# A hand-kept order table of 1,528 operations is replaced by another, with other engines for some of them

## Chip, core and metric

The kernel runs on one core of one Trainium2 chip. The metric is device time in microseconds (us), the median of several executions. Five engines matter: TensorE (PE, with PEld for its weight loads), VectorE (DVE), ScalarE (ACT), GpSimd (POOL) and the DMA queue of SyncE (SP).

## The reference, cut to what matters

Attention over chunks of 32 queries with 16 keys to the left, 8 to the right and 8 memory keys, for 4 batches of 8 heads, followed by a feed-forward block with a gate made by a 3-tap convolution over the sequence:

```python
scores = scale * np.matmul(q_c, k_full.transpose(0, 1, 3, 2))
a = np.exp(scores - np.max(scores, axis=-1, keepdims=True))
a = a / (np.sum(a, axis=-1, keepdims=True) + 1e-09)
out[:, :, c_start:c_end] = np.matmul(a, v_full)
...
h = np.maximum(x @ w_in, 0.0)                      # 512 -> 1024
conv_out = sum(conv_w[k] * hp[:, k:k + S, :] for k in range(3))
gate = 1.0 / (1.0 + np.exp(-conv_out))
return (h * gate @ w_out).astype(np.float32)       # 1024 -> 512
```

q is 4 x 8 x 768 x 64. The weights arrive as 64-bit floats in the kernel's buffers and are split on the chip into a rounded high part and a low part.

## The kernel before, in words

Everything stays in one recorded plan. `attention(n)` records the work of one of 32 pieces (4 batches x 2 halves of the sequence x 4 pairs of heads; "piece 20" below is n = 20): three loads, 24 score matmuls into PSUM tile `s` (L381), a maximum on VectorE (L390), the softmax, a sum and its reciprocal (L422, L424), a normalising multiplication (L427), a turn of the weights (three transposes on TensorE, L439, with copies L446, or a VectorE transpose L457 with two DMAs), 24 value matmuls into `ta` (L486), and the split of the result into a high part (ACT L489) and a low part (DVE L492).

`ffn_in(b, fc, hf)` multiplies the four results of a half by one block of 128 channels of `w_in`, as hi*hi + lo*hi + hi*lo, three matmuls of 384 columns each (L508), into a PSUM tile `f`, which ACT empties with a relu (L518). Four such tiles exist. `gated(b, fc)` makes the gate of a channel block ("block 1,6" is batch 1, fc 6): the middle tap (L528 on ACT or L532 on DVE), two more taps on DVE (L537, 128 x 767), a sigmoid on ACT (L541), the multiplication h * gate (L545 on DVE or GpSimd), a rounded high part (ACT L549) and the low part (L552 on DVE or GpSimd). `ffn_out(b, tt)` multiplies all eight blocks of a batch by `w_out` (L564) and stores the rows (L575 and a DMA). `from_f64` splits the weights (L276 to L348) in one of several kinds, chosen by a letter.

Which engine takes an optional operation stands in strings with one letter for each piece or block. `TAP` (A or V) is the middle tap, `MULT` and `LO` (V = VectorE, G = GpSimd) are L545 and L552, `NORM` is L427, `SOFT` is V for one VectorE subtraction (L395) and one ACT exponential (L401), or A for a small VectorE scaling (L407) and six ACT exponentials (L413). `W_IN`, `W_OUT` and `W_CONV` are the kinds of split. `KEEP` and `HOME` choose buffers.

The list `ORDER` gives the sequence in which the recorded operations are emitted. Each engine runs its own instructions in that sequence and waits where an operand or a buffer is not ready. Nothing is reordered on the chip. A buffer goes to the operation that comes next in `ORDER` once the last user of the buffer has been emitted. The numbers in `ORDER` are places in the recording, so the list moves whole operations, their DMAs included. No planner runs in the kernel: the arguments `cost`, `shared`, `late`, `gap` and so on of `Plan.op` are not read when the plan runs. `shared=True` marks what the author took to use the port that VectorE and GpSimd have in common: L280, L286, L293, L301, L306, L312, L348, L407, L427, L532, L537, L545, L552.

Of the kernel before, what the change touches and what calls it, by code (L numbers as in the profile page):

```python
# [29 lines left out]
W_IN, W_OUT, W_CONV = "SMMSmMCM", "CmMMCMMM", "R"  # L30
TAP = "AAAAAAVAAAAAAAAAAVAVAVAAVAAAAAAA"
MULT = "VGGVGGGGGVGGGGGGVVGVVVVVVGVGVVGG"
LO = "VGGVVVVVVVGGGGVGVVVGGVGVVGGGGVVG"
SOFT = "AVVAAAAVAVVAVVVAVVVAVVVVVVAAAVAV"
NORM = "GGVVGGVGGGGGVGGGVVVGVVVVVGVGVVGV"
KEEP = "KKKKKNNKKKKKKNKKNKKNNKKNKNKNNNNK"
HOME = "wwwwwwwwwwwwwwwwwwxxwwwwwxxxwxxx"
# [73 lines left out]
]  # L111


# [578 lines left out]
```

## Time and profile before

| what | value |
|---|---|
| three executions | 362.62, 363.25, 363.29 us, median 363.25 |
| the profiled execution | 362.65 us, of which the span of its instructions is 360.9 us |
| PE busy | 339.0 us (94%) in 2955 matmuls |
| DVE busy | 255.5 us (71%) in 431 instructions |
| ACT busy, POOL busy | 215.5 us (60%), 100.4 us (28%) |
| granted TensorE clock, mean | 0.995 |

The profiled execution lies 1.75 us above its span and 0.6 us under the median. Shares of busy time are averages over stages with different limits: VectorE is nearly always busy in the first 200 us and almost idle in the last 45, and TensorE is the reverse. So the windows have to be read by stage. A matmul's end is modelled, so "PE busy" in a window says where TensorE waited and not how fast it ran.

### The profile page before, as it was taken

The page shows a single profiled execution, that of the slowest core. Times are in us where ns is not written, and L with a number is a line of the kernel's source. Part 1 is how long each engine was busy: PE and PEld are TensorE (multiplying, and loading weights), DVE is VectorE, ACT ScalarE, POOL GpSimd, SP SyncE. Part 2 cuts the span into 40 slices and gives each one's busy share as a digit, 9 for nine tenths or more (in the row PEclk, how much of TensorE's full clock was granted, in tenths as well). Part 3 has the DMA queues.
Part 4 walks back from the last instruction along what each step waited for, and adds up shares of the span by engine and source line. Part 5 has one row for each costly group of instructions (what it writes and reads, how often), then busy time and mean ns, then how long its engine had stood idle before and what let it go on. Part 6 is the DMA issues. An engine that isn't in the chain of part 4 may idle for free.

```text
span 360.9 us, 7378 instructions
## 1 busy us (share of the span) xinstructions
PE 339.0 (94%) x2955; PEld 299.6 (83%) x2955; DVE 255.5 (71%) x431; ACT 215.5 (60%) x401; POOL 100.4 (28%) x75
## 2 busy tenths in 40 slices
PE   1799999999989978799999999999999999999996
PEld 1679899879979977789988789988998888888886
DVE  4999999999999999999999828350645997300000
ACT  2567888699988958755749786322579623311011
POOL 3314121292424355520002064000004596400000
PEclk9999999999999999899999999999999999999999
DMA  8998947866748545352065383512000110201012
GB/s 287 404 396 279 345 153 250 256 216 218 251 143 261 184 141 205 98 174 91 0 226 184 122 255 111 171 58 91 2 0 0 40 53 26 88 29 58 31 58 87
DMA packets 26386, 54.50 MB, mean 151 GB/s; under 512 B 3056, under 2 KB 13168, under 8 KB 26352
## 3 DMA queue, kind: packets, MB, share of 16 engines
q1 hardware_dynamic: 26352, 54.04, 44.2%
q8 instruction: 23, 0.38, 0.4%
q14 instruction: 11, 0.09, 0.1%
HBM read 44.79 MB, written 9.24 MB: 150 GB/s over the span
## 4 chain that ended last, share of the span: by engine, by line
PE 58%; DVE 22%; issue 2%; ACT 2%; POOL 0%; ACTq 0%; POOLq 0%; DVEq 0%
PE f L564 38%; PE f L508 16%; DVE w L537 9%; PE ta L486 2%; PE s L381 2%; DVE u L492 1%; DVE top L390 1%; DVE z L422 1%; DVE e L395 1%; DVE e L427 1%; DVE w L457 1%; DVE u L545 1%; DVE w L306 1%; DVE w L301 1%; DVE w_top L286 1%
## 5 line engine op out<-in xcount | busy, mean ns | idle before, releaser
L508 PE MATMUL f<-u,w_in_hi 128*128 128x384 f32 x512 | 143.9, 347 | 4.6 <-DVE u L492 3.1
L564 PE MATMUL f<-w_out_hi,u 128*128 128x512 f32 (+1 forms) x400 | 125.7, 388 | 0.0
L508 PEld LDWEIGHTS f<-u,w_in_hi 128*128 128x128 f32 x512 | 94.0, 190 | 9.9 <-DVE u L492 5.0
L564 PEld LDWEIGHTS f<-w_out_hi,u 128*128 128x128 f32 x400 | 74.1, 188 | 16.0
L508 PE MATMUL f<-u,w_in_lo 128*128 128x384 f32 x256 | 86.8, 339 | 0.0
L537 DVE SCALAR_TENSOR_TENSOR w<-u,cw,w 128x767 f32<-128x767 f32 x64 | 80.6, 1268 | 4.1 <-ACT w L528 3.3
L564 PE MATMUL f<-w_out_lo,u 128*128 128x512 f32 (+1 forms) x200 | 77.2, 386 | 0.0
L575 ACT COPY w_top<-f 128x512 f32<-128x512 f32 (+1 forms) x25 | 14.3, 570 | 61.0 <-PE f L564 60.4
L508 PEld LDWEIGHTS f<-u,w_in_lo 128*128 128x128 f32 x256 | 48.7, 190 | 0.7
L518 ACT ACTIVATE u<-f 128x384 f32<-128x384 f32 x64 | 30.6, 491 | 23.7 <-PE f L508 23.6
L564 PEld LDWEIGHTS f<-w_out_lo,u 128*128 128x128 f32 x200 | 37.6, 188 | 7.3
L545 POOL TENSOR_TENSOR u<-w,u 128x768 f32<-128x768 f32 x12 | 26.0, 2166 | 61.3 <-ACT w L541 59.4
L541 ACT ACTIVATE w<-w 128x768 f32<-128x768 f32 x32 | 26.9, 844 | 16.2 <-DVE w L537 16.1
L486 PEld LDWEIGHTS ta<-a_d,w 128*64 128x64 f32 x768 | 24.9, 140 | 5.6 <-ACT a_d L446 2.2
L486 PE MATMUL ta<-a_d,w 128*64 128x64 f32 x768 | 27.7, 227 | 1.9 <-ACT a_d L446 1.0
L427 POOL TENSOR_TENSOR e<-e,z 128x384 f32<-128x384 f32 x16 | 15.3, 958 | 45.8 <-DVE z L424 38.3
L528 ACT ACTIVATE w<-u,cw 128x768 f32<-128x768 f32 x27 | 25.3, 937 | 3.7 <-PE s L381 2.1
L492 DVE TENSOR_TENSOR u<-ta,u 128x384 fp32r<-128x384 f32 x32 | 17.4, 548 | 12.0 <-ACT u L489 11.8
L381 PE MATMUL s<-k,w 128*64 128x64 f32 x672 | 24.7, 227 | 1.0 <-DVE e L395 1.0
L381 PEld LDWEIGHTS s<-k,w 128*64 128x64 f32 x672 | 22.1, 141 | 4.2 <-DVE e L395 1.8
L545 POOL TENSOR_TENSOR w<-w,u 128x768 f32<-128x768 f32 x6 | 13.1, 2188 | 40.0 <-ACT w L541 40.0
L552 POOL TENSOR_TENSOR u<-u,u 128x768 fp32r<-128x768 f32 x9 | 19.2, 2143 | 15.5 <-ACT u L549 14.1
(62 smaller groups left out, 368.7 us busy)
## 6 DMA issues: line engine op xcount, KB each, us to landing
w<-in_v_dram SPq DMA_DIRECT2D x32, 384.0 KB, 5.2
w<-in_q_dram SPq DMA_DIRECT2D x28, 384.0 KB, 4.6
k<-in_k_dram SPq DMA_DIRECT2D x28, 252.0 KB, 4.9
out_dram<-w_top SPq DMA_DIRECT2D x23, 256.0 KB, 2.0
w<-in_w_in_dram SPq DMA_DIRECT2D x8, 512.0 KB, 6.9
w<-in_w_out_dram SPq DMA_DIRECT2D x8, 512.0 KB, 4.1
t_dram<-w SPq DMA_DIRECT2D x15, 192.0 KB, 2.1
a_d<-t_dram SPq DMA_DIRECT2D x30, 96.0 KB, 3.3
```

The source lines that it names most:

```text
L381: nc.tensor.matmul(s.t[j * D : (j + 1) * D, o : o + KW], lhsT=q_[:, c], rhs=k_t.t[:, c * STEP : c * STEP + KW], start=True, stop=True,)
L427: lambda: (V if norm == "V" else G).tensor_tensor(out=keys(e), in0=keys(e), in1=pairs(z.t).unsqueeze(3).broadcast_to([P, NG, 2, KW]), op=A ...
L486: nc.tensor.matmul(y, lhsT=v_g[:, g, u, h], rhs=a_d.t[:, :, o], start=True, stop=True)
L492: lambda: V.tensor_tensor(out=x.t[:, TW:S], in0=a.t[:, :TW], in1=x.t[:, :TW].bitcast(F32), op=ALU.subtract), (a, (x, 0)), ((x, 1),),
L508: nc.tensor.matmul(f.t[:, :TW], lhsT=w_in_p[c][:, fc, cc], rhs=x.t[:, a * TW : (a + 1) * TW], start=(cc == 0 and i == 0), stop=(cc == NCC ...
L518: "A", act(TW, True), lambda: A.activation(h.t[:, hf * TW : (hf + 1) * TW], f.t[:, :TW], AF.Relu), (f,), ((h, hf),)
L528: plan.op("A", act(S, ptr=1), lambda: A.activation(c.t, h.t, AF.Copy, scale=w[1]), H, (c,))
L537: lambda j=j, to=to, at=at: V.scalar_tensor_tensor(out=c.t[:, to], in0=h.t[:, at], scalar=w[j], in1=c.t[:, to], op0=ALU.mult, op1=ALU.add) ...
L541: plan.op("A", act(S), lambda: A.activation(c.t, c.t, AF.Sigmoid), (c,), (c,), table="sigmoid")
L545: lambda: (V if mult == "V" else G).tensor_tensor(out=y.t, in0=c.t, in1=h.t, op=ALU.mult), (c, h), (y,), shared=True,
L552: lambda: (V if lo == "V" else G).tensor_tensor(out=g_lo.t, in0=y.t, in1=g_hi.t.bitcast(F32), op=ALU.subtract),
L564: nc.tensor.matmul(ps.t[:, :n], lhsT=gs[b, fc][a].t[:, tt * P : (tt + 1) * P], rhs=w_out_p[c][:, fc, o : o + n], start=(fc == 0 and i == 0 ...
```

## The change

All letters that choose engines and kinds, and the whole of `ORDER`, are replaced. In the letters: `W_IN` block 1 goes from M to C (its low part moves from DVE to ACT and GpSimd) and block 6 from C to M, block 4 no longer uses GpSimd for one step; the split of `conv_w` changes (one operation fewer). `SOFT` goes from 13 to 10 A, `TAP` from 5 to 7 V, `MULT` from 18 to 19 G, `LO` from 15 to 13 G, `NORM` stays at 16 G. On each engine that is: VectorE 431 to 435 operations, GpSimd 61 to 59, ScalarE 316 to 313; ScalarE's queue holds 24 loads of a function table instead of 20, and two of the four more stand before the turned weights of piece 20. TensorE's 2955 matmuls and the DMAs are the same in number and shape, in another order. `gap=380` becomes `gap=460`, an argument that nothing reads.

```diff
-W_IN, W_OUT, W_CONV = "SMMSmMCM", "CmMMCMMM", "R"
-TAP = "AAAAAAVAAAAAAAAAAVAVAVAAVAAAAAAA"
-MULT = "VGGVGGGGGVGGGGGGVVGVVVVVVGVGVVGG"
-LO = "VGGVVVVVVVGGGGVGVVVGGVGVVGGGGVVG"
-SOFT = "AVVAAAAVAVVAVVVAVVVAVVVVVVAAAVAV"
-NORM = "GGVVGGVGGGGGVGGGVVVGVVVVVGVGVVGV"
-KEEP = "KKKKKNNKKKKKKNKKNKKNNKKNKNKNNNNK"
-HOME = "wwwwwwwwwwwwwwwwwwxxwwwwwxxxwxxx"
+W_IN, W_OUT, W_CONV = "SCMSMMMM", "CmMMCMMM", "s"
+TAP = "AAAAAAVAAAVAAAAAAAVVAAAAAVAVAVAA"
+MULT = "VGGVGGGGGVVGGGGGVVGVGGGGVVGGVVVV"
+LO = "VGGGVVVVGVGVGGVGGVGVVVGGVVVVVGVV"
+SOFT = "VVVAAAAVVAVAVVVAVVVAVVVVVVVAVAVV"
+NORM = "VGVGGGGGVGGGVGGGVVVGVVVVVGVVVGGV"
+KEEP = "KKKKKNNKKKKKKNKKNKKNNKKNKKNNKNKN"
+HOME = "wwwwwwwwwwxwwwwwwwxxwwwwwxxxwxxx"
...
 ORDER = [
-    571, 12, 13, 581, 30, 29, 81, 47, 46, 572, 573, 64, 574, 63, 575, 15, 576, 577, 591, 582, 16, 14, 17, 587, 18, 583, 80,
...
+    570, 11, 12, 580, 28, 29, 45, 46, 571, 62, 572, 80, 573, 574, 63, 14, 575, 576, 591, 581, 586, 577, 15, 13, 16, 79, 582,
...
-    def op(self, eng, cost, do, r=(), w=(), shared=False, table=None, mode=None, late=70, gap=380, less=None):
+    def op(self, eng, cost, do, r=(), w=(), shared=False, table=None, mode=None, late=70, gap=460, less=None):
```

**Place A, VectorE's queue at the gates of batch 1.** Names are buffers; `w_90<-u_1269` is a pair of taps of block 1,4, then come 1,3 (`u_1204`), 1,6 (`u_1292`) and 1,5 (`u_1372`). Before:

```order
L537 SCALAR_TENSOR_TENSOR w_90<-u_1269,cw,w_90 128x767 x2
L286 TENSOR_SCALAR w_top_101<-w_top_101 128x512
L492 TENSOR_TENSOR u_1615<-ta_113,u_1615 128x384
L390 TENSOR_REDUCE top_104<-s_112 128x6
L537 SCALAR_TENSOR_TENSOR w_86<-u_1204,cw,w_86 128x767 x2
L492 TENSOR_TENSOR u_1654<-ta_114,u_1654 128x384
L395 TENSOR_TENSOR e_76<-s_112,top_104 128x3x128
L537 SCALAR_TENSOR_TENSOR w_87<-u_1292,cw,w_87 128x767 x2
L390 TENSOR_REDUCE top_105<-s_111 128x6
L395 TENSOR_TENSOR e_74<-s_111,top_105 128x3x128
L537 SCALAR_TENSOR_TENSOR w_90<-u_1372,cw,w_90 128x767 x2
```

The same place after the change (block 1,4 is `u_1229`, 1,3 is `u_1210`, 1,6 is `u_1366`; `u_1433` is block 1,2):

```order
L537 SCALAR_TENSOR_TENSOR w_86<-u_1229,cw,w_86 128x767
L537 SCALAR_TENSOR_TENSOR w_91<-u_1210,cw,w_91 128x767
L545 TENSOR_TENSOR u_1433<-w_92,u_1433 128x768
L390 TENSOR_REDUCE top_103<-s_111 128x6
L492 TENSOR_TENSOR u_1644<-ta_114,u_1644 128x384
L492 TENSOR_TENSOR u_1649<-ta_113,u_1649 128x384
L537 SCALAR_TENSOR_TENSOR w_91<-u_1210,cw,w_91 128x767
L537 SCALAR_TENSOR_TENSOR w_92<-u_1366,cw,w_92 128x767
L395 TENSOR_TENSOR e_76<-s_111,top_103 128x3x128
L390 TENSOR_REDUCE top_105<-s_112 128x6
L395 TENSOR_TENSOR e_75<-s_112,top_105 128x3x128
L537 SCALAR_TENSOR_TENSOR w_92<-u_1366,cw,w_92 128x767
```

The two taps of a block no longer stand together: the second tap of one block is followed by the first of the next and then by two or three attention operations, and the multiplication of block 1,2 is now in this queue.

**Place B, GpSimd's queue from the last step of batch 1 on.** L545 are multiplications, L552 low parts, L427 a normalisation. Before (the first row is the weight step that follows block 1,7):

```order
L343 TENSOR_TENSOR w_out_lo<-w_97 128x512
L552 TENSOR_TENSOR u_1873<-u_463,u_1576 128x768
L552 TENSOR_TENSOR u_1927<-u_606,u_1868 128x768
L545 TENSOR_TENSOR u_1940<-w_86,u_1940 128x768
L427 TENSOR_TENSOR e_74<-e_74,z_110 128x3x128
L552 TENSOR_TENSOR u_2407<-u_1269,u_2392 128x768
L552 TENSOR_TENSOR u_2453<-w_90,u_2331 128x768
L427 TENSOR_TENSOR e_74<-e_74,z_107 128x3x128
L552 TENSOR_TENSOR u_2568<-u_1435,u_2467 128x768
```

After, from the same step:

```order
L343 TENSOR_TENSOR w_out_lo<-w_97 128x512
L552 TENSOR_TENSOR u_1869<-u_465,u_1541 128x768
L552 TENSOR_TENSOR u_1914<-u_596,u_1905 128x768
L552 TENSOR_TENSOR u_1938<-u_524,u_1928 128x768
L545 TENSOR_TENSOR u_1890<-w_90,u_1890 128x768
L545 TENSOR_TENSOR w_92<-w_92,u_1797 128x768
L545 TENSOR_TENSOR u_1825<-w_89,u_1825 128x768
L427 TENSOR_TENSOR e_75<-e_75,z_110 128x3x128
L545 TENSOR_TENSOR u_1810<-w_90,u_1810 128x768
L552 TENSOR_TENSOR u_2377<-w_86,u_2362 128x768
L552 TENSOR_TENSOR u_2414<-u_1240,u_2168 128x768
L552 TENSOR_TENSOR u_2467<-u_1293,u_2453 128x768
```

One more low part stands at the front, and then four multiplications of batch 2 instead of one, in a row but for a normalisation; a fifth (block 2,4) is the next row.

## Rows read from the trace of the kernel before

**Rows 1.** The page: busy time of the engines, and the last chain's shares.

```profile
PE 339.0 (94%) x2955; PEld 299.6 (83%) x2955; DVE 255.5 (71%) x431; ACT 215.5 (60%) x401; POOL 100.4 (28%) x75
PE 58%; DVE 22%; issue 2%; ACT 2%; POOL 0%; ACTq 0%; POOLq 0%; DVEq 0%
```

**Rows 2.** Windows: their length, then busy PE, PEld, DVE, ACT, POOL, clock, DMA share, GB/s.

```profile
9.00:18.00 9.00, 6.62 (x84) 5.46 (x86) 8.62 (x19) 4.98 (x13) 3.15 (x4) 1.00 1.04 402
...
126.00:135.00 9.00, 7.19 (x79) 6.62 (x79) 8.93 (x9) 4.95 (x9) 4.51 (x2) 1.00 0.44 137
135.00:144.00 9.00, 7.50 (x67) 6.73 (x63) 8.80 (x11) 7.72 (x12) 4.90 (x2) 1.00 0.60 208
144.00:153.00 9.00, 7.04 (x34) 6.41 (x33) 8.58 (x18) 6.37 (x11) 4.33 (x3) 0.84 0.35 105
```

**Rows 3.** The chain that ended last: start, length, what.

```profile
145.81 1.87 DVE e L427
...
149.76 0.39 ACT u L518
150.19 4.95 PE f L508 x18
...
269.50 88.28 PE f L564 x402
```

**Rows 4.** VectorE's groups, 54 to 150 us: count, busy us, mean ns, idle before.

```profile
L537 DVE SCALAR_TENSOR_TENSOR w<-u,cw,w 128x767 f32<-128x767 f32 x32 | 42.3, 1326 | 0.4
...
L395 DVE TENSOR_TENSOR e<-s,top 128x384 f32<-128x384 f32 x11 | 6.1, 551 | 0.1
L427 DVE TENSOR_TENSOR e<-e,z 128x384 f32<-128x384 f32 x6 | 4.6, 772 | 0.1
...
L293 DVE SCALAR_TENSOR_TENSOR w_top<-w,w_top 128x512 uint32<-128x512 uint32 x5 | 3.4, 685 | 0.0
L545 DVE TENSOR_TENSOR u<-w,u 128x768 f32<-128x768 f32 x3 | 3.3, 1101 | 0.0
L301 DVE TENSOR_SCALAR w<-w 128x512 uint32<-128x512 uint32 x4 | 3.2, 794 | 0.0
...
L286 DVE TENSOR_SCALAR w_top<-w_top 128x512 uint32<-128x512 uint32 x4 | 2.6, 644 | 0.0
```

**Rows 5.** VectorE's groups, 153 to 211 us, where GpSimd runs six instructions.

```profile
L537 DVE SCALAR_TENSOR_TENSOR w<-u,cw,w 128x767 f32<-128x767 f32 x16 | 16.0, 1009 | 0.6 <-ACT w L528 0.4
...
L545 DVE TENSOR_TENSOR u<-w,u 128x768 f32<-128x768 f32 x3 | 2.9, 950 | 0.0
...
L286 DVE TENSOR_SCALAR w_top<-w_top 128x512 uint32<-128x512 uint32 x3 | 1.3, 417 | 0.0
```

**Rows 6.** Timeline at blocks 1,3 and 0,7: start, length, instruction, idle before.

```profile
130.16 0.84 ACT L541 ACTIVATE w<-w 128x768 f32<-128x768 f32 x1 [1.60 <-DVE w L537]
...
130.97 3.56 DVE L537 SCALAR_TENSOR_TENSOR w<-u,cw,w 128x767 f32<-128x767 f32 x2
...
131.08 2.64 POOL L545 TENSOR_TENSOR u<-w,u 128x768 f32<-128x768 f32 x1 [2.82 <-ACT w L541]
...
99.77 1.83 POOL L545 TENSOR_TENSOR u<-w,u 128x768 f32<-128x768 f32 x1
```

**Rows 7.** VectorE's groups in the first 27 us.

```profile
L348 DVE SCALAR_TENSOR_TENSOR w_in_lo<-w 128x512 fp32r<-128x512 uint32 x2 | 2.5, 1249 | 0.0
```

**Rows 8.** Timeline up to batch 3's first matmul, and later at alternating multiplications.

```profile
188.51 0.63 PE L564 MATMUL f<-w_out_hi,u 128*128 128x512 f32 x2
...
210.59 0.56 DVE L492 TENSOR_TENSOR u<-ta,u 128x384 fp32r<-128x384 f32 x1 [1.03 <-ACT u L489]
...
213.57 0.34 PE L508 MATMUL f<-u,w_in_hi 128*128 128x384 f32 x1
...
291.39 2.60 DVE L537 SCALAR_TENSOR_TENSOR w<-u,cw,w 128x767 f32<-128x767 f32 x1
```

**Rows 9.** ScalarE's timeline at the sigmoid of block 1,5.

```profile
139.12 1.28 ACT L541 ACT_TABLE_LOAD   x1 [0.20 <-DVE w L537]
```

134 rows, old and new, of the table ORDER are left out of this document.

## The prediction

> **What bounds the kernel now.** I read the page's busy line and chain first, then the windows, then VectorE by groups and by time. TensorE is busy 339.0 of 360.9 us and its matmuls stay the same, so only the time in which it waits can be won [rows 1]. The chain's shares, PE 58% and DVE 22%, say that there are two stages [rows 1]. The second is simple: from 150.19 us on every piece of the chain is TensorE's until the last copy, ending in one run of 402 matmuls in 88.28 us [rows 3]. Whatever TensorE has lost by then moves the end by as much.
>
> In the first stage TensorE waits for VectorE. VectorE is busy 8.6 to 8.9 of 9 us in the windows shown, while TensorE has 6.62 at the start and 7.19, 7.50 and 7.04 from 126 to 153 us [rows 2]. Those three late windows alone lack 27 - 21.73 = 5.3 us. After the last of the waits the clock fell too: 0.84 granted in 144 to 153 us, so part of that window ran at 1.2 and not 2.4 GHz [rows 2]. The chain shows the last link: VectorE's normalisation of piece 20 at 145.81 takes 1.87 us, ScalarE's relu follows two instructions later, and it frees the `f` tile for the matmul at 150.19 [rows 3].
>
> So VectorE's time up to piece 20 sets the end. Part of that time is no work. Its tap L537 takes 1326 ns in the mean of 32 between 54 and 150 us, and 1009 ns in the mean of 16 in a stretch where GpSimd runs six instructions only [rows 4, 5]. The timeline shows why. The sigmoid of block 1,3 starts at 130.16 and takes 0.84; GpSimd's multiplication starts at 131.08, gets the port after the tap then running, and takes 2.64 instead of 1.83; and the pair of taps takes 3.56 instead of 2.02, the second having waited 1.5 us [rows 6]. L395, which reads PSUM, keeps its 551 ns [rows 4].
>
> **The change, part by part.** I make the sum at the place where TensorE waits for piece 20's normalisation, and then follow it to batch 3.
>
> *Work on VectorE up to there.* Its queue has 263 instructions up to that row before and 268 after. One more each: the multiplication of block 1,2 (L545, 0.95 [rows 5]), L395 (0.55 [rows 4]), L390 (same size as L395, 0.55), L293 and L325 (0.69 each [rows 4]) and a tap L532, which I take at L293's 0.69; a small L407 falls away. That is 4.1 us, less some 0.6 because neighbours in the queue overlap by up to a tenth: 3.5. TensorE has one group of three matmuls less ahead of the same place, under 0.22 each by the long run [rows 3], so it arrives 0.5 earlier and waits for that too. Together **+4.0 us**.
>
> *Waiting for the port, 54 to 150 us.* Before: L537 32 x (1326 - 1009) = 10.1, L427 6 x (772 - 551) = 1.3, L301 4 x (794 - 417) = 1.5, L286 4 x (644 - 417) = 0.9, L545 3 x (1101 - 950) = 0.5 (short times from the rows with little GpSimd; L301 has L286's size) [rows 4, 5]: 14.3 us, with 22 GpSimd instructions. For after I go along place A with a sigmoid and two handoffs (1.0 us from the end of the second tap, as 130.1 to 131.08 [rows 6]) and 1.83 for GpSimd. After block 1,4's second tap comes the first of 1,3 and the multiplication of 1,2, both under way before GpSimd asks; it gets the port at 1.9; then stand L390 and two L492, 1.5 us that need no port; the next tap waits 0.35. At block 1,3 one tap, then L395, L390, L395: 0.4. At 1,6 a table load of 1.28 [rows 9] delays the sigmoid past the first tap of 1,5, and 0.7 remains. Before, each of these three places lost 1.5, and block 1,2 another 1.5, which is now on VectorE. Going in this way through all 21 GpSimd instructions of the stretch I get 9 us. The least would be 4, if every reduction that stands near were to cover; the most 14.3 x 21/22 = 13.7, the rate of before. I take 9: **-5.2 us**.
>
> *The first 27 us.* L348 took 1249 ns twice where its neighbours of the same size take 685 [rows 4, 7], because of GpSimd's steps of the first two weight blocks. In the new order attention's reductions stand behind those steps. TensorE has 6.62 of 9 us there [rows 2] and waits for VectorE or for transfers, whose order is nearly the same. I take **-1.0 us**, between 0 and -2.
>
> At piece 20 that makes 4.0 - 5.2 - 1.0 = -2.2 us.
>
> *Batch 2's multiplications, 153 to 213 us.* This stage has GpSimd nearly free before: six instructions against 16 taps at 1009 ns [rows 5]. After the change place B puts seven between the last part of `w_out` and the result of piece 24 (L492): four multiplications, a normalisation, two low parts. VectorE's queue holds 35 instructions in that piece (40 before), about 18 us by the rows, less overlaps. By the walk of place A the waits are 0.3, 1.2, 1.6, 0.4, 1.3 and 1.4, so 6.2 us, and 8.0 if block 2,5's multiplication is late. That gives 24.2 to 26 us, plus 0.5 for odd waits on other engines. TensorE's matmuls in that piece took 188.75 to 213.57 = 24.8 us, and then VectorE had finished L492 2.4 us ahead, after an idle stretch [rows 8]. So the margin goes, and TensorE waits 0 to 1.7 us at batch 3's first matmul: **+0.6 us**.
>
> *ScalarE.* Two more table loads up to piece 20 are 2 x 1.28 = 2.6 us [rows 9]; the queue loses a tap, two weight steps and six exponentials there, and it is the less busy engine (4.95, 7.72 and 6.37 of 9 us [rows 2]). Cost 0, covered by its idle time; 2.6 if that cover is gone. The Trainium skill, in ScalarE: Activation LUTs, What ACT_TABLE_LOAD costs, puts a switch at 2.66 us, a drain of 1.38 after the load included; the sum would then have 5.3 us of ScalarE time to hide in place of 2.6. No row here is read as showing such a drain.
>
> *What costs nothing.* `gap` is not read. Behind batch 3's start VectorE idles for much of the time, and its last low parts come earlier relative to the matmuls. The last matmuls, copy and store keep their sizes. Buffers (`KEEP`, `HOME`) and the order of loads move too; loads run far ahead after 30 us, so I put 0, between -0.5 and +1.
>
> Sum: -2.2 + 0.6 = -1.6; 362.65 - 1.6 = 361.0 us, against the profiled execution, which lies 0.6 under the median of 363.25.
>
> **Rivals.**
>
> *Slower: the port costs as much per GpSimd instruction as before.* The walk rests on the moment at which sigmoids end. Before, reductions stood behind the pairs of taps as well and yet did not cover, because GpSimd came in between the two taps of a pair [rows 6]. If ACT's queue shifts those moments by half a microsecond, the cover is missed again; then only 0.6 of the 14.3 us goes and the larger VectorE work decides: 4.0 - 0.6 - 0.5 = +2.9, and 0.5 for the clock that falls after longer waits: 366.0. It decides from 12.5 us of port waits on (4.0 + 12.5 - 14.3 - 1.0 = +1.2, over the median's bound).
>
> *No change: batch 3's start takes the gain back.* In a later stretch where GpSimd has one multiplication after another, every port-taking VectorE instruction takes 2.6 us, as L537 at 291.39 [rows 8], so 1.6 each is lost. Four multiplications in a row in place B could do that to five instructions, 8 us and more, and 2.5 us of waiting at batch 3: 362.65 - 2.2 + 2.5 = 363.0. The Trainium skill, in SBUF — State Buffer, Who interferes with whom, says that whoever of the two engines starts first holds the shared pair for its whole instruction while the other blocks; by that rule alone this alternation is what a filled GpSimd queue must bring, and the trace agrees in the pair of 3.56 us.
>
> *Faster by much: the covers hold.* Port waits of 5 us in the first stage and 4 in the second: 4.0 - 9.3 - 1.0 = -6.3, of which batch 3's start lets through 5: 357.6.
>
> **How the numbers follow.** Chances: my forecast, 361.0 with its own bounds 359.5 to 362.5, 0.47; slower, 366.0, 0.24; no change, 363.0, 0.16; much faster, 357.6, 0.13. The range takes half of each outer case: 358.0 to 365.3. About 0.2% (0.7 us) is what a measurement here can tell from no change: faster means under 362.5, 0.47 + 0.13 = 0.60; within, 0.16; slower, 0.24.
>
> **What would show it.** In the profile after: L537's mean between 54 and 150 us at about 1180 ns and not 1326 if the walk is right, and no pair of 3.5 us at blocks 1,4 and 1,3; L537's mean from 153 to 211 us above 1009, near 1300; TensorE's busy time from 126 to 153 us up by about 2 us; a wait of TensorE for VectorE or ScalarE near 210 us where none was; the run of TensorE in the chain beginning there and not at 150. The forecast is wrong if L537's mean in the first stage stays above 1270, or if TensorE waits for loads or for ScalarE after 60 us.

## The result, and the profile after

The changed kernel takes 358.67 us (median of four, 356.15 to 358.82) against 363.10: ratio 0.987, 95% interval 0.983 to 0.991. Taken again beside other runs of the kernel before (363.02), it took 357.90, ratio 0.986 (0.984 to 0.988). It is faster by some 4.4 to 5.1 us. The forecast of 361.0 was 2.3 us too high by the first figure, which lies 0.7 us inside the range of 358.0 to 365.3, and 3.1 too high by the second, which lies 0.1 us below it. The profiled execution is the shortest of them, 356.15 us with a span of 354.4, so its rows show less loss than the median has.

The page's busy line of the kernel after, beside [rows 1]: VectorE has four instructions more and is busy 6.2 us less.

```profile
PE 337.0 (95%) x2955; PEld 298.4 (84%) x2955; DVE 249.3 (70%) x435; ACT 216.7 (61%) x387; POOL 95.2 (27%) x73
```

The windows of the kernel after, in the columns of [rows 2]:

```profile
9.00:18.00 9.00, 5.51 (x76) 4.70 (x76) 8.53 (x21) 4.79 (x9) 3.67 (x4) 1.00 1.03 403
126.00:135.00 9.00, 9.00 (x111) 8.68 (x110) 8.87 (x15) 8.65 (x11) 3.88 (x3) 1.00 0.58 205
135.00:144.00 9.00, 8.82 (x51) 8.12 (x50) 8.80 (x16) 8.93 (x15) 4.47 (x3) 1.00 0.44 144
144.00:153.00 9.00, 7.15 (x77) 6.11 (x75) 8.60 (x14) 6.22 (x13) 6.13 (x4) 1.00 0.30 93
```

From 126 to 144 us TensorE hardly waits any more (0.18 us); VectorE is as full as before. One of these late windows has a long wait left, 144 to 153. The window from 9 to 18 us has 1.1 us less of TensorE time, and the next one, 18 to 27, gives 0.9 of it back (9.00 after, 8.11 before).

Over the whole profile TensorE is busy 97.10 us between 60 and 160 us, where it was 91.96, and 48.55 us in the first 60, where it was 49.23. So 5.1 us of waiting went behind 60 us and 0.7 came ahead of it. The other 2.0 of the 6.5 us between the two spans is the busy time of the same matmuls, 337.0 and not 339.0 us. Most of that is the clock: before, 0.84 was granted in 144 to 153 us [rows 2] and 0.97 in the next 9 us, which makes (0.16 + 0.03) x 9 = 1.7 us, an estimate.

VectorE's groups of the kernel after, 54 to 150 us, as in [rows 4]:

```profile
L537 DVE SCALAR_TENSOR_TENSOR w<-u,cw,w 128x767 f32<-128x767 f32 x32 | 33.7, 1074 | 0.4
...
L427 DVE TENSOR_TENSOR e<-e,z 128x384 f32<-128x384 f32 x8 | 6.8, 844 | 0.2
L293 DVE SCALAR_TENSOR_TENSOR w_top<-w,w_top 128x512 uint32<-128x512 uint32 x6 | 6.2, 1039 | 0.1
...
L545 DVE TENSOR_TENSOR u<-w,u 128x768 f32<-128x768 f32 x4 | 4.3, 1098 | 0.0
...
L280 DVE TENSOR_SCALAR w_top<-w_top 128x512 f32<-128x512 f32 x4 | 2.4, 602 | 0.0
```

By the short times of [rows 4, 5] the waits for the port are now 32 x 0.065 + 8 x 0.293 + 6 x 0.354 + 4 x 0.148 + 4 x 0.185 = 7.9 us, where they were 14.3 and 9 was forecast. (L280 takes L286's 417 as its short time.) L537's mean is 1074, under the 1180 that the forecast named. The waits have moved: from the taps to L427 and L293. L395, one operand of which is in PSUM, has a mean of 549 ns, as before (551).

VectorE's and GpSimd's timelines of the kernel after at blocks 1,4 and 1,3 (place A), as in [rows 6]:

```profile
124.86 0.55 DVE L390 TENSOR_REDUCE top<-s 128x6 f32<-128x384 f32 x1
125.33 1.01 DVE L492 TENSOR_TENSOR u<-ta,u 128x384 fp32r<-128x384 f32 x2
126.25 2.15 DVE L537 SCALAR_TENSOR_TENSOR w<-u,cw,w 128x767 f32<-128x767 f32 x2
128.33 0.55 DVE L395 TENSOR_TENSOR e<-s,top 128x384 f32<-128x384 f32 x1
128.80 0.54 DVE L390 TENSOR_REDUCE top<-s 128x6 f32<-128x384 f32 x1
129.37 0.56 DVE L395 TENSOR_TENSOR e<-s,top 128x384 f32<-128x384 f32 x1
...
124.22 2.44 POOL L545 TENSOR_TENSOR u<-w,u 128x768 f32<-128x768 f32 x1 [7.83 <-ACT w L541]
128.44 1.86 POOL L545 TENSOR_TENSOR u<-w,u 128x768 f32<-128x768 f32 x1 [1.78 <-ACT w L541]
```

GpSimd's second multiplication lasts from 128.44 to 130.30, and L395, L390 and L395 of VectorE stand in that time, each at its usual 0.55. None of the three is held up. The pair of taps ahead takes 2.15 where [rows 6] had 3.56, and no pair of 3.5 us is left.

The last wait of TensorE in the kernel after (timelines of VectorE, GpSimd and TensorE):

```profile
140.86 0.60 DVE L427 TENSOR_TENSOR e<-e,z 128x384 f32<-128x384 f32 x1
...
145.45 2.13 DVE L427 TENSOR_TENSOR e<-e,z 128x384 f32<-128x384 f32 x1
...
148.19 1.95 DVE L293 SCALAR_TENSOR_TENSOR w_top<-w,w_top 128x512 uint32<-128x512 uint32 x1
...
150.77 1.01 DVE L492 TENSOR_TENSOR u<-ta,u 128x384 fp32r<-128x384 f32 x2
...
145.33 1.83 POOL L552 TENSOR_TENSOR u<-u,u 128x768 fp32r<-128x768 f32 x1
147.74 1.85 POOL L552 TENSOR_TENSOR u<-u,u 128x768 fp32r<-128x768 f32 x1 [0.58 <-POOL u L552]
...
151.84 0.44 PE L508 MATMUL f<-u,w_in_hi 128*128 128x384 f32 x1 [1.85 <-DVE u L492]
```

Piece 20's normalisation, the place of the forecast's sum, ends at 141.46 and not at 147.68 [rows 3]. TensorE waits ten microseconds later, for L492, the low part of an attention result. Beside two low parts on GpSimd, L427 and L293 ahead of it are 1.58 and 1.27 us longer than their short times.

### The profile page after: what moved, and what is told of

Its sections match the earlier page's. It is cut to its first block, busy times and chain, and to the rows that moved or that the text cites. A ratio compares the mean times of both kernels' runs of the same rounds, so it can differ in the third digit from the quotient of the medians.

```text
span 354.4 us, 7367 instructions
## 1 busy us (share of the span) xinstructions
PE 337.0 (95%) x2955; PEld 298.4 (84%) x2955; DVE 249.3 (70%) x435; ACT 216.7 (61%) x387; POOL 95.2 (27%) x73
## 4 chain that ended last, share of the span: by engine, by line
PE 56%; DVE 24%; issue 1%; DMA 1%; ACT 0%; DVEq 0%; ACTq 0%
PE f L564 38%; PE f L508 14%; DVE w L537 8%; PE ta L486 2%; DVE z L422 2%; PE s L381 2%; DVE u L492 2%; DVE e L427 2%; DVE e L395 1%; DVE w_top L293 1%; DVE top L390 1%; DVE u L545 1%; DVE w L457 1%; DVE w L306 1%; DVE w_top L280 1%
## 5 line engine op out<-in xcount | busy, mean ns | idle before, releaser
L537 DVE SCALAR_TENSOR_TENSOR w<-u,cw,w 128x767 f32<-128x767 f32 x64 | 72.0, 1146 | 7.3 <-ACT w L528 6.8
L575 ACT COPY w_top<-f 128x512 f32<-128x512 f32 (+1 forms) x25 | 14.1, 569 | 57.9 <-PE f L564 55.3
L518 ACT ACTIVATE u<-f 128x384 f32<-128x384 f32 x64 | 31.0, 488 | 24.0 <-PE f L508 23.8
L545 POOL TENSOR_TENSOR u<-w,u 128x768 f32<-128x768 f32 x12 | 24.6, 2050 | 57.9 <-ACT w L541 57.9
L545 POOL TENSOR_TENSOR w<-w,u 128x768 f32<-128x768 f32 x7 | 14.8, 2110 | 45.0 <-ACT w L541 45.0
L427 POOL TENSOR_TENSOR e<-e,z 128x384 f32<-128x384 f32 x16 | 15.6, 975 | 36.2 <-DVE z L424 34.8
L528 ACT ACTIVATE w<-u,cw 128x768 f32<-128x768 f32 x25 | 23.2, 934 | 3.1 <-issue 1.8
L492 DVE TENSOR_TENSOR u<-ta,u 128x384 fp32r<-128x384 f32 x32 | 17.2, 546 | 10.2 <-ACT u L489 10.2
L390 DVE TENSOR_REDUCE top<-s 128x6 f32<-128x384 f32 x32 | 17.1, 543 | 8.1 <-PE s L381 8.1
```

The source lines that it names most:

```text
L390: lambda: V.tensor_reduce(out=pairs(top.t), in_=s_(), axis=AX.X, op=ALU.max), (s,), (top,),
L427: lambda: (V if norm == "V" else G).tensor_tensor(out=keys(e), in0=keys(e), in1=pairs(z.t).unsqueeze(3).broadcast_to([P, NG, 2, KW]), op=A ...
L492: lambda: V.tensor_tensor(out=x.t[:, TW:S], in0=a.t[:, :TW], in1=x.t[:, :TW].bitcast(F32), op=ALU.subtract), (a, (x, 0)), ((x, 1),),
L518: "A", act(TW, True), lambda: A.activation(h.t[:, hf * TW : (hf + 1) * TW], f.t[:, :TW], AF.Relu), (f,), ((h, hf),)
L528: plan.op("A", act(S, ptr=1), lambda: A.activation(c.t, h.t, AF.Copy, scale=w[1]), H, (c,))
L537: lambda j=j, to=to, at=at: V.scalar_tensor_tensor(out=c.t[:, to], in0=h.t[:, at], scalar=w[j], in1=c.t[:, to], op0=ALU.mult, op1=ALU.add) ...
```

## Experiments

| run | median us | ratio to before, 95% |
|---|---|---|
| changed kernel, again | 357.90 | 0.984 to 0.988 |
| before, GpSimd's part cut | 348.90 | 0.959 to 0.962 |
| changed, GpSimd's part cut | 351.79 | 0.967 to 0.970 |
| before, three pairs of taps split | 360.79 | 0.991 to 0.996 |
| changed, normalisation first | 356.68 | 0.980 to 0.984 |
| changed, low parts on VectorE | 355.05 | 0.976 to 0.981 |
| changed, multiplication 1,2 back | 358.28 | 0.985 to 0.990 |
| changed, batch 2's multiplications back | 357.73 | 0.983 to 0.989 |
| new order, old engines | 357.81 | 0.984 to 0.988 |
| old order, new engines | 364.43 | 1.004 to 1.006 |
| low parts and normalisation | 355.21 | 0.979 to 0.982 |
| the same, sums before the weight step | 356.98 | 0.982 to 0.985 |

The first theory: the gain is the time that VectorE waits for the port, less the larger work that the change gives it. Its rival: the gain is elsewhere, in ScalarE's, the loads' or TensorE's order.

**The changed kernel again**, with no edit.

> The changed kernel once more, for a second profile and an interval on this chip. The profiled execution after the change took 356.15 us with a granted clock of 1.000 in the mean, the four others 358.5 to 358.8 with 0.986 to 0.995. If the 2.6 us between them is a fall of the clock after a wait of TensorE, this profile (if it takes about 358.8) shows a window with a clock under 1 and TensorE's lateness growing there by some 2.5 us, and is like the first profile before it. If it is something else (loads, for example), the lateness grows elsewhere, at full clock.

A window of this run, and the same one in the first profile of the changed kernel:

```profile
153.00:162.00 9.00, 9.00 (x81) 8.15 (x81) 7.26 (x14) 3.75 (x8) 0.37 (x1) 0.83 0.58 215
```

```profile
153.00:162.00 9.00, 9.00 (x87) 7.85 (x87) 8.60 (x17) 5.23 (x11) 0.51 (x1) 1.00 0.62 217
```

The wait ahead of it is the same, 1.9 us for L492, but behind it the granted clock is 0.83, so part of the window ran at 1.2 and not 2.4 GHz: TensorE does 81 matmuls in it, not 87. At 145 us this execution is 0.16 us ahead of the first one (L427 starts at 145.29 and at 145.45), and at 160 us it is 1.25 behind, so 1.4 us were lost in between; the span is 355.7 against 354.4 us. So this wait costs 1.9 us, and in some executions over 1 us more. That is half of the 2.6 us that the expectation asks about; no profile shows the other half. The clock was also low between 9 and 27 us in this run (0.90, then 0.73), which cost nothing that is left at 145 us.

**Both kernels with GpSimd's part cut.** GpSimd's multiplications and normalisations (L545, L427) touch 24 columns and not all; the rest of that arithmetic is left out. Orders and waits stay.

```diff
-            lambda: (V if norm == "V" else G).tensor_tensor(
+            lambda: V.tensor_tensor(
...
+            ) if norm == "V" else G.tensor_tensor(
+                out=e.t[:, 0, 1:25], in0=e.t[:, 0, 1:25], in1=z.t[:, :1].broadcast_to([P, 24]), op=ALU.mult
...
-            lambda: (V if mult == "V" else G).tensor_tensor(out=y.t, in0=c.t, in1=h.t, op=ALU.mult), (c, h), (y,), shared=True,
+                out=y.t[:, :S if mult == "V" else 24], in0=c.t[:, :S if mult == "V" else 24],
+                in1=h.t[:, :S if mult == "V" else 24], op=ALU.mult), (c, h), (y,), shared=True,
```

> The kernel before, with GpSimd's multiplications (L545) and normalisations (L427) cut to 24 columns, the order untouched. It leaves out most of that arithmetic, so the output is not the reference's. Theory (the waits for the port set the first stage): the 14.3 us of port waits between 54 and 150 us fall under 2, L537's mean there is near 1020 ns, and the time falls by 8 to 13 us, to about 350 to 355. Rival (another engine or the order itself sets it): L537 gets short but the time falls by under 4 us.

> The changed kernel with the same cut of GpSimd's L545 and L427 (most of that arithmetic left out). Theory: with no port to wait for, the changed kernel keeps only its larger VectorE work (3.5 us more up to piece 20), so it is slower than the cut kernel before by 1 to 4 us: the whole gain of the change is port waits. Rival (the new order is better in itself, by what stands ahead on TensorE, ScalarE or the queues): it is still faster than the cut kernel before by 2 us or more.

The kernel before falls by 363.02 - 348.90 = 14.1 us, a little more than the 8 to 13 expected; the changed one falls by 357.90 - 351.79 = 6.1, and now the changed one is 2.9 us slower, as expected. The taps between 54 and 150 us take 1013 and 1009 ns, so their port waits are gone. TensorE waits nowhere behind 60 us in either. The windows up to 60 us and behind, first before, then changed, both cut:

```profile
0.00:60.00 60.00, 49.44 (x643) 45.33 (x644) 51.90 (x130) 41.28 (x105) 13.39 (x31) 1.00 0.85 302
60.00:340.00 280.00, 280.00 (x2281) 249.29 (x2280) 181.36 (x302) 173.06 (x295) 46.20 (x44) 1.00 0.40 128
```

```profile
0.00:60.00 60.00, 47.72 (x630) 42.41 (x630) 51.67 (x127) 38.08 (x96) 12.07 (x30) 1.00 0.84 306
60.00:340.00 280.00, 279.97 (x2275) 248.85 (x2274) 187.57 (x309) 176.23 (x289) 38.92 (x43) 1.00 0.39 126
```

So with GpSimd's part cut the change loses 2.9 us, and with that part whole it wins 5.1: the 8.0 us between the two are what the change saves of GpSimd's cost. The cut also shortens GpSimd itself, so the 8.0 is not the port alone; but the rival that the gain comes from elsewhere has fallen: all waits of TensorE behind 60 us in the kernel before hang on GpSimd's part, and with that part away the change gains nothing. That the change saves these waits through VectorE's queue is shown by a run for 2.2 us (the next one); for the rest it is read from the timelines. The 2.9 us are not VectorE's larger work on the way to piece 20. Behind 60 us TensorE is full in both cut kernels, so more work of VectorE there delays nothing. Of the 2.7 us between the two profiled spans (347.2 and 349.9), 1.7 are waits in the first 60 us, and 1.0 is the busy time of the same matmuls (333.5 and 334.5 us).

**The kernel before with three pairs of taps split**, engines and kinds unchanged: taps of blocks 1,3, 1,6 and 1,5 each moved apart, with attention's operations between. VectorE's queue:

```diff
+L537 SCALAR_TENSOR_TENSOR w_86<-u_1204,cw,w_86 128x767
 L492 TENSOR_TENSOR u_1615<-ta_113,u_1615 128x384
 L390 TENSOR_REDUCE top_104<-s_112 128x6
-L537 SCALAR_TENSOR_TENSOR w_86<-u_1204,cw,w_86 128x767 x2
+L537 SCALAR_TENSOR_TENSOR w_86<-u_1204,cw,w_86 128x767
+L537 SCALAR_TENSOR_TENSOR w_87<-u_1292,cw,w_87 128x767
...
```

> The kernel before with six VectorE operations moved in its order and nothing else: at blocks 1,3, 1,6 and 1,5 the pair of attention operations that stood ahead of the two taps now stands between them, as at place A after the change. Engines and kinds as before. Theory: three of the port waits of 1.5 us fall to about 0.4, L537's mean between 54 and 150 us falls from 1326 to about 1220 ns, and the time falls by 2 to 4.5 us (359 to 361). Rival (the gain comes from the new choice of engines, or a wait is only moved): within 1 us of before.

The taps of this run from 54 to 150 us (group):

```profile
L537 DVE SCALAR_TENSOR_TENSOR w<-u,cw,w 128x767 f32<-128x767 f32 x32 | 40.2, 1267 | 0.3
```

Two of its pairs (VectorE's timeline):

```profile
127.86 2.62 DVE L537 SCALAR_TENSOR_TENSOR w<-u,cw,w 128x767 f32<-128x767 f32 x2
...
131.33 2.78 DVE L537 SCALAR_TENSOR_TENSOR w<-u,cw,w 128x767 f32<-128x767 f32 x2
```

2.62 and 2.78, where such pairs took 3.56 [rows 6]. 2.2 us are won by moving six VectorE operations, and the queues of the other engines keep their order. The mean fell to 1267, not to the 1220 I had named, so the moves covered about half of the port waits that they were meant to cover.

**Order or engines.** The changed kernel's order table with the engine letters of before, and the other way round; both complete.

```diff
-MULT = "VGGVGGGGGVVGGGGGVVGVGGGGVVGGVVVV"
-LO = "VGGGVVVVGVGVGGVGGVGVVVGGVVVVVGVV"
-NORM = "VGVGGGGGVGGGVGGGVVVGVVVVVGVVVGGV"
+MULT = "VGGVGGGGGVGGGGGGVVGVVVVVVGVGVVGG"
+LO = "VGGVVVVVVVGGGGVGVVVGGVGVVGGGGVVG"
+NORM = "GGVVGGVGGGGGVGGGVVVGVVVVVGVGVVGV"
```

> The changed kernel with its order table and its kinds of operations, but with the engines of the kernel before for every multiplication (MULT), low part (LO) and column normalisation (NORM); nothing is left out. Theory (the order is what keeps VectorE's port operations from standing back to back beside GpSimd's; which operation runs on which engine is worth 1 us at most): L537 between 54 and 150 us keeps a mean of 1070 to 1150 ns, and the time is 357 to 360 us. Rival (the engine choice carries the gain): L537 back at 1250 ns or more, 361 to 364 us.

> The kernel before with its order table and its kinds of operations, but with the changed kernel's engines for every multiplication (MULT), low part (LO) and column normalisation (NORM); nothing is left out. Theory (the order carries the gain): the pairs of taps of 3.5 us at blocks 1,3 and its neighbours stay, L537 between 54 and 150 us stays between 1270 and 1350 ns, and with 1 us more on VectorE in the first stage the time is 362 to 366 us. Rival (the engine choice carries it): 358 to 360.5 us.

The taps from 54 to 150 us with the new order and old engines:

```profile
L537 DVE SCALAR_TENSOR_TENSOR w<-u,cw,w 128x767 f32<-128x767 f32 x32 | 35.3, 1123 | 0.4
```

And with the old order and new engines:

```profile
L537 DVE SCALAR_TENSOR_TENSOR w<-u,cw,w 128x767 f32<-128x767 f32 x32 | 40.6, 1275 | 0.4
```

Two pairs of taps in the timeline of that run:

```profile
122.17 2.06 DVE L537 SCALAR_TENSOR_TENSOR w<-u,cw,w 128x767 f32<-128x767 f32 x2
...
130.46 3.56 DVE L537 SCALAR_TENSOR_TENSOR w<-u,cw,w 128x767 f32<-128x767 f32 x2
```

And one in the run with the new order and the old engines:

```profile
122.86 3.54 DVE L537 SCALAR_TENSOR_TENSOR w<-u,cw,w 128x767 f32<-128x767 f32 x2
```

The order with the old engines takes 357.81 us, as little as the whole change; the engines with the old order take 364.43, 1.9 more than before in that comparison (362.56). So the order carries the gain. The pairs of taps follow it only in part. The kernel before has four of 3.5 us, which start at 121.89, 126.61, 130.97 and 135.51 us. With the old order and the new engines the first is short (2.06) and the others stay at 3.32 to 3.56; with the new order and the old engines the first is long again (3.54) and the others are gone. So the first pair goes with the engines and the other three with the order. The letters W_IN, W_CONV, TAP, SOFT, KEEP and HOME went with the order; how much of the gain is theirs stays open.

**One multiplication undone.** Block 1,2's multiplication back on GpSimd (the eleventh letter of MULT from V to G).

> The changed kernel with one of its parts undone: the multiplication (L545) of block 1,2 on GpSimd again, not on VectorE, in the same place of the order. Theory (the prediction's term: VectorE pays 0.95 us for it, and on GpSimd it costs VectorE a port wait only if a tap stands beside it): where it stands, near 120 us, VectorE is 5 to 9 us ahead of TensorE's need at the changed kernel's pace, so within 0.5 us of the changed kernel either way; GpSimd's queue moves 0.9 us back. Rival (the move of this one multiplication is what broke the alternation of the two engines at the gates of batch 1): the pairs of taps of 3.5 us come back at blocks 1,4 and 1,3, the mean of L537 between 54 and 150 us goes from 1074 back above 1200 ns, and 2 us or more are lost.

358.28 us, no measurable difference from 357.90 and 358.67. L537 rose to 1123 ns, 32 x 0.049 = 1.6 us, and VectorE had 0.95 less to do: the two nearly cancel. One pair of 3.5 us came back, that at block 1,4:

```profile
123.53 3.55 DVE L537 SCALAR_TENSOR_TENSOR w<-u,cw,w 128x767 f32<-128x767 f32 x2
```

The two pairs behind it stayed at 2.15 and 2.19 us, the mean stayed under the 1200 ns of the rival, and no time was lost. So the rival is right about one pair, and the gain does not rest on it.

**Batch 2's multiplications undone** (letters 21 to 24 of MULT from G to V).

> The changed kernel with the multiplications (L545) of blocks 2,4 to 2,7 on VectorE again, not on GpSimd, in the same place of the order. Theory (behind 152 us TensorE never waits again, so nothing that VectorE or GpSimd do there sets the end): L537 between 153 and 211 us goes from a mean of 1282 ns back to about 1010 to 1060, the normalisation of piece 24 ends within 1 us of where it was, and the time is within 0.4 us of the changed kernel. Rival (the prediction's term: these multiplications on GpSimd make VectorE late at the start of batch 3, and cost 0.6 us): 0.4 to 0.8 us faster than the changed kernel.

357.73 us, no difference. Its taps from 153 to 211 us take 1165 ns in the mean; those of the changed kernel:

```profile
L537 DVE SCALAR_TENSOR_TENSOR w<-u,cw,w 128x767 f32<-128x767 f32 x16 | 20.3, 1282 | 1.4 <-ACT w L528 1.3
```

The mean fell less than expected (1010 to 1060). The time did not care: TensorE does not wait there.

**The last wait, from two sides.** First, L492 ahead of L293 on VectorE. L492 is the low part of the attention results of pieces 21 and 20; the expectation calls it their normalisation.

```diff
 L457 STREAM_TRANSPOSE w_97<-e_74 128x6x2x32
+L492 TENSOR_TENSOR u_1909<-ta_114,u_1909 128x384
+L492 TENSOR_TENSOR u_1913<-ta_113,u_1913 128x384
+L419 MEMSET e_76 64x8
+L422 TENSOR_REDUCE z_107<-e_76 128x6
 L293 SCALAR_TENSOR_TENSOR w_top_101<-w_99,w_top_101 128x512
...
```

> The changed kernel with one move in its order table, the engines as they are: the normalisation of pieces 21 and 20 (L492, two operations on VectorE) stands ahead of the weight step L293 and of a small MEMSET and TENSOR_REDUCE, not behind them. In the unchanged one L492 starts at 150.6 us, behind L293, which took 1.97 us instead of 0.68 beside GpSimd's L552; TensorE's last wait for VectorE ends at 151.71 us after 1.86 us. Theory (this wait is all that the first stage still costs, and everything after it runs at TensorE's pace): L492 then starts at about 148.2 and ends at 149.3, ahead of the 149.7 us at which TensorE asks for it; the wait goes, and about 1 us more where the clock fell behind it, so 1.9 to 3 us less than the changed kernel: 355 to 356.5 us. Rival (the wait only moves: L293 feeds the weights of batch 3, and comes 1 us later, or the next rows of VectorE are as late): within 0.5 us of the changed kernel, 357.5 to 358.7 us, with a wait of TensorE of over 1 us between 150 and 160 us for another operation.

356.68 us: 1.2 to 2.0 us won, just short of what was expected (1.9 to 3, to 356.5 at most). The wait moved. ScalarE's timeline in this run:

```profile
151.72 0.62 ACT L298 CAST w_out_hi<-w_top 128x512 fp32r<-128x512 f32 x1 [2.15 <-DVE w_top L293]
```

TensorE's largest wait behind 60 us in it (sum, times, longest):

```profile
PE f L508 <- ACT u L518: 2.0, 3, 1.5
```

ScalarE stood 2.15 us before L298, a cast that needs the delayed L293, and the ReLU (L518) that TensorE needs stood behind it. Both theories were half right.

Second, the low parts of blocks 0,1 and 0,2 on VectorE, order unchanged:

```diff
-LO = "VGGGVVVVGVGVGGVGGVGVVVGGVVVVVGVV"
+LO = "VVVGVVVVGVGVGGVGGVGVVVGGVVVVVGVV"
```

> The changed kernel with the low parts (L552) of blocks 0,1 and 0,2 on VectorE, not on GpSimd, in the same place of the order. There they ran on GpSimd from 145.2 to 147.0 and from 147.6 to 149.5 us, and VectorE's L427 and L293 beside them took 2.13 and 1.97 us instead of 0.60 and 0.68. Theory (VectorE loses at the port what a GpSimd instruction lasts, wherever a port operation of VectorE stands beside it): 2.8 us of port waits go, two operations of about 1.0 us come, L492 ends about 0.8 us earlier, TensorE's wait at 149.7 us falls from 1.9 to about 1.1: 0.5 to 1.5 us less than the changed kernel. Rival (the model's choice of engines is best as it stands: the operations cost VectorE as much as the waits): within 0.4 us.

VectorE's timeline in this run:

```profile
145.81 0.56 DVE L427 TENSOR_TENSOR e<-e,z 128x384 f32<-128x384 f32 x1
146.28 0.95 DVE L552 TENSOR_TENSOR u<-u,u 128x768 fp32r<-128x768 f32 x1
...
147.65 0.65 DVE L293 SCALAR_TENSOR_TENSOR w_top<-w,w_top 128x512 uint32<-128x512 uint32 x1
...
149.80 1.01 DVE L492 TENSOR_TENSOR u<-ta,u 128x384 fp32r<-128x384 f32 x2
```

Its window behind that place:

```profile
153.00:162.00 9.00, 9.00 (x89) 8.14 (x88) 8.26 (x17) 5.60 (x10) 0.00 (x0) 1.00 0.60 211
```

355.05 us, 2.9 to 3.6 less than the changed kernel, and the lowest of the runs whose computation is whole. Two operations of 0.95 us came, 2.85 us of port waits went, and L492 starts 0.97 us earlier, as reckoned. TensorE's wait for it is 0.50 us now, so 1.35 us of it went. The gain in the median is twice the 0.5 to 1.5 expected. Between the two profiles in which the clock behind the wait is 1.00, this one and the first of the changed kernel, it is 354.4 - 353.2 = 1.2 us, as expected. The rest is what the changed kernel's other executions take more than its first profile; the fall of the clock behind the wait is 1.4 us of that in the one that was traced.

Both moves together, with ScalarE's L298 behind that ReLU, and then also piece 22's sums (L424, L427) ahead of L293:

> The changed kernel with both moves that concern its last wait: the low parts (L552) of blocks 0,1 and 0,2 on VectorE, and the normalisation of pieces 21 and 20 (L492) ahead of the second of them and of the weight step L293. ScalarE's cast of that weight step's result (L298) now stands behind the ReLU (L518) that TensorE waits for; in the run with the normalisation moved alone it stood ahead of it and held it up by 2.15 us. Theory (TensorE then waits nowhere behind 120 us): the remaining wait of 0.5 us at 150.9 us goes, no new one over 0.3 us comes between 145 and 165 us, and the time is 0.4 to 0.9 us under the run with the low parts alone (355.05 us): 354.2 to 354.7 us. Rival (ScalarE's cast for the weights of batch 3, now later, is what TensorE waits for next): 355 us or more.

> The kernel of the last run (low parts of blocks 0,1 and 0,2 on VectorE, normalisation of pieces 21 and 20 ahead) with one more move on VectorE: the weight step L293 stands behind the two operations of piece 22's column sums (L424, L427), not ahead of them. In the last run L293 took 1.63 instead of 0.68 us beside GpSimd's low part of block 0,3, L427 behind it ended at 153.5 us, and TensorE waited 1.0 us for it (L439). Theory (the operation that stands ahead of a needed one takes the port wait, so the needed one goes first; L424 does not use the port): L427 ends at about 152.2 us, TensorE's wait falls under 0.3 us, L293 comes 1 us later and nobody on the way to the end needs it: 354.0 to 354.8 us. Rival (the last run's wait hid another): a wait of 0.5 us or more for another operation between 150 and 165 us, 355 us or more.

355.21 and 356.98 us: no gain over the low parts alone, and the second is 1.9 us slower than they are; both theories failed. Each wait gave way to the next. With both moves, L293 stood beside GpSimd's next low part and took 1.63 us, and TensorE waited for the sums behind it; with the sums ahead, ScalarE waited 3.17 us for L293 and its copy (L446) came late. VectorE's timeline in the first, where TensorE's longest wait behind 60 us is 1.0 us, for that L427:

```profile
151.19 1.63 DVE L293 SCALAR_TENSOR_TENSOR w_top<-w,w_top 128x512 uint32<-128x512 uint32 x1
```

ScalarE's timeline in the second:

```profile
154.34 1.14 ACT L298 CAST w_out_hi<-w_top 128x512 fp32r<-128x512 f32 x2 [3.17 <-DVE w_top L293]
```

TensorE's largest wait in that one:

```profile
PE ta L486 <- ACT a_d L446: 1.0, 1, 1.0
```

The 1.8 us between the two are not this wait, which is as long in both. In its profile the second is already behind at 27 us (TensorE 14.29 us busy there against 14.88), although the two kernels are alike up to there: its first matmul starts at 7.96 and not at 6.12 us, behind the first transfer of k. Whether its other executions started late too is not known.

## Why the prediction was right, and where it was off

The direction held, and so did the mechanism: VectorE's port waits fell, because operations that the port does not hold up now stand beside GpSimd's. The size did not. A gain of 2.1 us was forecast from 363.10, and 4.4 to 5.1 were measured; the range held by 0.7 us in one measurement and missed by 0.1 in the other, so that the result lies inside it is in part luck. The rival "the covers hold" (357.6, given 0.13) was nearest.

*Waits for the port, 54 to 150 us, -5.2.* This term was mis-sized. Over the whole stretch it is 14.3 to 7.9, so -6.4, but up to piece 20's normalisation, where the sum was made, it is 14.3 to 4.3 (taps 2.1, L427 0.8, L293 0.9, L545 0.6), so -10.0: 3.6 us of the 7.9 stand behind that place (L280, L427 and L293). VectorE's windows from 54 us to the end of that normalisation, before and after:

```profile
54.00:147.68 93.68, 87.08 (x952) 80.75 (x950) 92.04 (x151) 78.99 (x132) 38.52 (x22) 1.00 0.66 211
```

```profile
54.00:141.46 87.46, 86.01 (x950) 80.41 (x949) 85.61 (x157) 80.75 (x137) 32.57 (x22) 1.00 0.67 218
```

The walk was too high at the places it went through itself: it gave 0.35 and 0.4 us to the taps behind the multiplications of blocks 1,4 and 1,3, and the two pairs there lost 0.13 (2.15 against 2.02) and 0.17. And it did not single out the two rows from 145 to 150 us, 2.85 us, which made the last wait.

*VectorE's work, +4.0.* About right. VectorE is busy 92.04 us in the first window and 85.61 in the second, 6.4 less; as 10.0 of port waits went, its work grew by 3.6, an estimate, where 3.5 was forecast for VectorE.

*The place of the sum.* Piece 20's normalisation ends 6.2 us earlier, where -2.2 was forecast, and nearly all of the difference is the port term. The "covers hold" rival has -6.3 there. But it no longer was what TensorE waited for: the last wait stands ten microseconds on, at L492, and gave back 1.9 us, and in some executions the clock's fall. That wait was in no term.

*The first 27 us, -1.0.* Wrong in sign. TensorE's waits in the first 60 us sum to 11.2 us after and 10.7 before. The wait at L348 did go (one instruction of 0.69 us is left in the first 27 us), but another came. VectorE, GpSimd and TensorE of the kernel after:

```profile
10.64 1.76 DVE L293 SCALAR_TENSOR_TENSOR w_top<-w,w_top 128x512 uint32<-128x512 uint32 x1
...
10.45 1.42 POOL L336 TENSOR_TENSOR w_in_lo<-w_top,w_in_hi 128x512 fp32r<-128x512 f32 x1 [1.07 <-ACT w_in_hi L333]
...
14.87 0.87 PE L439 MATMUL ta<-ident,e 128*128 128x128 f32 x3 [2.22 <-DVE e L427]
```

GpSimd's L336 now starts at 10.45 and stands in front of VectorE's L293, whose short time is 0.69; piece 0's normalisation comes behind it. I had looked at the operation that lost its wait and not at what GpSimd's step would meet where it went.

*Batch 3's start, +0.6.* It did not come. The taps there take 1282 ns, as said (near 1300). TensorE reaches batch 3's first matmul 6.5 us earlier than before and VectorE's result only 4.6, so the margin shrank, and just held. VectorE and TensorE of the kernel after:

```profile
206.04 0.55 DVE L492 TENSOR_TENSOR u<-ta,u 128x384 fp32r<-128x384 f32 x1
...
207.04 0.34 PE L508 MATMUL f<-u,w_in_hi 128*128 128x384 f32 x1
```

The result is there 0.45 us ahead; [rows 8] had 2.4. Taking the multiplications back changed nothing. The no-change rival needed 2.5 us of waiting here and has fallen, by a margin of half a microsecond.

*ScalarE, 0.* Right: TensorE's waits for it behind 60 us sum to 0.2 us. The drain behind a table load, which the prediction quotes, is not in the trace of the kernel before: the load of [rows 9] ends at 140.40, and the sigmoid starts there:

```profile
140.41 0.85 ACT L541 ACTIVATE w<-w 128x768 f32<-128x768 f32 x1
```

The slower rival (366.0) needed 12.5 us of port waits; 7.9 were left. The old order with the new engines, at 364.43, is the nearest that the runs come to the change without the covers.

## What to carry to other kernels

When two engines share a port, look at what stands on the one just when the other asks: operations that the port does not hold up (here reductions and reads of PSUM) took no longer there. Moving six of them in the old kernel was worth 2.2 us, and the whole new order with its kinds of operations 4.8, while the choice of engine for multiplications, low parts and normalisations was worth nothing measurable in the new order and cost 1.9 us in the old one. Price a wait where it falls: taking away the 2.9 us of port waits just ahead of TensorE's last wait won 2.9 us or more of the median, while TensorE's other waits behind 60 us sum to 0.7 us, although 5 us of port waits were left elsewhere. And when an instruction is moved out of the way, ask what it meets at its new place and which engine's queue stands behind it.

## What I had not expected of the hardware

A wait of TensorE of 1.85 us can cost more than itself. Of the five profiles in the new order with that wait (the changed kernel twice, the two engine undoings 1,2 and batch 2, the new order with old engines), three have a granted clock of 0.81 to 0.83 in the 9 us behind it and two have 1.00. With the wait at 0.5 us the clock behind it stayed at 1.00, and so it did with waits of 1.0 and 1.5 us. What decides between the two at the same wait stays open.

GpSimd's low part (1.83 us) held L427, whose short time is 0.55, for 1.58 us and L293 (0.69) for 1.27; L395, L390 and L492, which stood beside GpSimd's multiplications, kept their 0.55.
